# Zero columns beside a weight tile, so that every pass of p @ v loads 128 columns

## The chip, the core and the metric

The kernel runs on one core of a Trainium2 chip. The metric is the device time of one execution in microseconds (us); lower is better. TensorE multiplies matrices: it loads a tile of weights (LDWEIGHTS, shown in the profile as the engine PEld) and then streams a moving operand through it (MATMUL, shown as PE) into an accumulator in PSUM. VectorE (DVE), ScalarE (ACT) and GpSimd (POOL) work element by element, and SyncE (SP) issues the DMA transfers.

## The reference: windowed attention, then a softplus feed-forward

Inputs are q, k and v of shape (8, 8, 576, 64) and two weight matrices, all float32.

```python
scores = scale * np.matmul(q, k.transpose(0, 1, 3, 2))
mask = (rel >= 0) & (rel < 64)              # rel = query position - key position
attn = softmax(np.where(mask, scores, -1e9))
x = np.matmul(attn, v)                      # heads side by side: (4608, 512)
h = x @ w_in                                # 512 -> 2048
out = softplus(h) @ w_out                   # 2048 -> 512
```

A query sees its own key and the 63 before it, so a tile of 128 queries needs 192 keys.

## The kernel before

**Blocks and groups.** The 4608 tokens are cut into 12 blocks (*groups*) of 384 tokens (three tiles of 128). A sequence has 576 tokens, so some groups start a sequence and have no keys before them (`prev` is false). The attention of a group runs over four *head pairs* `hp`; each pair has two heads `hh` of 64 columns. The feed-forward of a group runs over 16 tiles `f` of the hidden width: `ffn_up` makes 12 products into `ps_h` (L403), softplus follows on ScalarE and VectorE (L407 to L414), and `ffn_down` makes 9 products into `ps_o` (L424). Both multiply float32 numbers that are split into two parts, three products of parts to each full one.

**Attention.** Groups 0 and 1 (in the kernel's own order) transpose the probabilities on TensorE and do everything in float32 (L255, L291, L349). The other ten groups, the ones that the change touches, go another way. Scores are products of split q and k (L259, four to a tile of queries). VectorE adds the mask and takes the minimum (L266), and ScalarE takes the exponential (L276). The probabilities p are divided by their sum (L284), then written as three bfloat16 parts p1 + p2 + p3 in the tile `nat` (L304 to L312), and two DMA transposes turn them into `tr` (L308, L313), which has keys on the partitions.

**p @ v in bfloat16 parts.** v is split in the same way, v1 + v2 + v3. Keys go through in chunks of 64, and 128 partitions hold a chunk twice. There are two sets of passes, `s = 0` and `s = 1`:

- `s = 0`: the moving operand has p1 in the upper 64 partitions and p2 in the lower ones. The weights `v12` have v1 in 64 columns and v2 in the 64 beside them, in both halves of the partitions. So the accumulator `av` gets (p1 + p2) v1 in its partitions 0 to 63, and (p1 + p2) v2 in partitions 64 to 127.
- `s = 1`: the moving operand has p3 above and p1 below. The weights `v13` have v1 above (L331) and v3 below (L330), in 64 columns. The result p3 v1 + p1 v3 belongs to partitions 0 to 63 alone, and before the change the product is written as a 64-column one.

A head has seven chunks (six where `prev` is false), so 14 (or 12) passes at L378, each with its own load of weights: over all, 80 heads, 1088 passes, half of them with `v13`. The inner chunks move 128 columns of `tr`, the first and the last chunk move 64. After the last pass, ScalarE and VectorE add the two halves of `av` (L383, L384), and the sum is split again into `x` (L386, L387), which `ffn_up` of the next group reads.

**What sets the order.** The stages of the attention are a generator; they and the steps of the feed-forward are put into one list of events with due times (`BASE`, `PACE`, `STG`, `DOWN`) and emitted in that order. Up to due time 100 a scheduler orders the instructions of every engine; from there on TensorE keeps the order in which the events were written, and the scheduler orders the other engines. In that part the 14 passes of a head stand together as a rule, and the four L259 products of a tile of the next head pair follow them.

Of the kernel before, what the change touches and what calls it, by code (L numbers as in the profile page):

```python
# [9 lines left out]
BF16 = mybir.dt.bfloat16  # L10
# [3 lines left out]
ALU = mybir.AluOpType  # L14

P = 128
# [5 lines left out]
NCH = TB // CH + 1  # L22
# [16 lines left out]
def window_attention_softplus_ffn(  # L39
# [24 lines left out]
    nc = tc.nc  # L64
# [11 lines left out]
    cpool = ctx.enter_context(tc.tile_pool(name="cpool", bufs=1))  # L76
    ld = ctx.enter_context(tc.tile_pool(name="ld", bufs=1))
    att = ctx.enter_context(tc.tile_pool(name="att", bufs=1))
# [35 lines left out]
    for t in kbd_s:  # L114
        nc.gpsimd.memset(t[D:P, 0, :], 0.0)
        nc.gpsimd.memset(t[0:D, 1, :], 0.0)
        nc.gpsimd.memset(t[0:D, 0, 0:CH], 0.0)
        nc.gpsimd.memset(t[D:P, 1, 0:CH], 0.0)
    v_pads = [att.tile([P, 2, NJ, 2, P], F32, name="v_pad", tag=n) for n in ("nat", "tr")]
    for t in v_pads:  # L120
        nc.vector.memset(t, 0.0)
# [59 lines left out]
    def attention(g, hp):  # L181
# [6 lines left out]
        def bank():  # L188
            if not odd0:
                return ps_a.tile([P, 512], F32, name="ps_a")  # L190

            taken_ps[0] += 1
            return ps_o.tile([P, 512], F32, name=f"ps_o{taken_ps[0] % NJ}")
# [40 lines left out]
        else:  # L234
            q_hl = att.tile([P, 2, TB], F32R, name="q_hl")
            low = heads[1]
# [48 lines left out]
        if by_pe:  # L285

            pt = att.tile([P, 2, TB], F32, name="pt", tag="q_hl")
            for hh in range(2):
                pp = bank()
                for j in range(NJ):  # L290
                    tp(pp[:, j * P : (j + 1) * P], sv[:, hh * NJ + j, 0:P], ident)  # L291
                (nc.vector.tensor_copy if hh else nc.scalar.copy)(pt[:, hh, :], pp[:, :TB])
        else:

            nat = att.tile([P, 2, 4 * NJ, 2, CH], BF16, name="nat")
            tr = att.tile([P, 8 * NJ, P], BF16, name="tr")
            pv = [pn.rearrange("p i (f c) -> p i f c", f=2), nat.rearrange("p s (i f) b c -> p s i f b c", f=2)]

            def part(s, b):
                return pv[1][:, s, :, :, b, :]  # L300

            n = 4 * NJ
            yield
            nc.scalar.copy(part(0, 0), pv[0])  # L304
            nc.vector.tensor_tensor(pv[0], pv[0], part(0, 0), ALU.subtract)  # L305
            yield
            nc.scalar.copy(part(0, 1), pv[0])  # L307
            nc.sync.dma_start(  # L308
                tr[:, 0:n, :], nat[:, 0, :, :, :].rearrange("p n b c -> p (n b c)"), transpose=True
            )  # L310
            nc.vector.tensor_tensor(part(1, 0), pv[0], part(0, 1), ALU.subtract)
            nc.vector.tensor_copy(nat[:, 1, :, 1, :], nat[:, 0, :, 0, :])  # L312
            nc.sync.dma_start(  # L313
                tr[:, n:, :], nat[:, 1, :, :, :].rearrange("p n b c -> p (n b c)"), transpose=True
            )
            yield
            v_in = att.tile([P, NCH, P], F32, name="v_in")
            for half in heads:
                nc.sync.dma_start(v_in[half, :, :], v[ks, c0 : c0 + P].rearrange("(c p) n -> p c n", p=CH))
            yield  # L320

            v12 = att.tile([P, NCH, 2, 2, D], BF16, name="v12")
            v13 = att.tile([P, NCH, 2, D], BF16, name="v13")
            vv = v_in.rearrange("p c (h d) -> p c h d", h=2)
            up, low = heads
            nc.scalar.copy(v12[:, :, :, 0, :], vv)  # L326
            nc.vector.tensor_tensor(vv, vv, v12[:, :, :, 0, :], ALU.subtract)  # L327
            yield
            nc.scalar.copy(v12[:, :, :, 1, :], vv)
            nc.vector.tensor_tensor(v13[low, :, :, :], vv[low, :, :, :], v12[low, :, :, 1, :], ALU.subtract)  # L330
            nc.vector.tensor_copy(v13[up, :, :, :], v12[up, :, :, 0, :])  # L331
        yield

        if hp == 0:
# [5 lines left out]
        if by_pe:  # L340
            av = bank()
# [3 lines left out]
        for hh in range(2):  # L345
            if by_pe:
                for a in range(2 * NJ):
                    cs = slice(a * CH, (a + 1) * CH)
                    mm(  # L349
                        av[:, cs], v_pad[:, a % 2, a // 2, hh, :], pt[:, hh, cs],  # L350
                        start=(hh == 0 and a == 0), stop=(hh == 1 and a == 2 * NJ - 1), skip_group_check=True,
                    )
                if hh == 1:
                    nc.scalar.copy(x_t[0], av[:, :TB])
                    nc.vector.tensor_tensor(x_t[1], av[:, :TB], x_t[0].bitcast(F32), ALU.subtract)
                yield
                continue
            av = bank()
            passes = []
            for s in range(2):  # L360
                for c in range(0 if prev else 1, NCH):


                    j = (c - 1) // 2
                    n = s * 4 * NJ + (hh * NJ + j) * 2
                    if c % 2:
                        src, o = trf[:, (n + 1) * P : (n + 2) * P], j * P
                    elif c == 0:
                        src, o = trf[:, (n + 2) * P : (n + 2) * P + CH], 0
                    elif c == NCH - 1:  # L370
                        src, o = trf[:, n * P + CH : (n + 1) * P], j * P + CH
                    else:
                        at = n * P + CH
                        src = trf[:, at : at + 2 * W].rearrange("p (a b) -> p a b", b=W)[:, :, 0:CH]
                        o = j * P + CH
                    passes.append((s, c, src, slice(o, o + (CH if c in (0, NCH - 1) else P))))
            for i, (s, c, src, osl) in enumerate(passes):
                mm(  # L378
                    av[: D if s else P, osl], v13[:, c, hh, :] if s else v12[:, c, hh, :, :], src,
                    start=(i == 0), stop=(i == len(passes) - 1), skip_group_check=True,  # L380
                )
            ds = heads[hh]
            nc.scalar.copy(xf[ds, :], av[D:P, :TB])  # L383
            nc.vector.tensor_tensor(xf[ds, :], av[0:D, :TB], xf[ds, :], ALU.add)  # L384
            if hh == 1:
                nc.scalar.copy(x_t[0], xf)  # L386
                nc.vector.tensor_tensor(x_t[1], xf, x_t[0].bitcast(F32), ALU.subtract)  # L387
            yield
# [68 lines left out]
    for g in range(NB):  # L457
        for hp in range(NP):
            if g < 3:
                base = BASE[g] + PACE[g] * hp  # L460
            else:
                base = 2 * NF * (g - 1) + SHP * hp + SH
            stages = attention(g, hp)
            for at in STG if g >= 2 else STG0:
                events.append((base + at, lambda stages=stages: next(stages, None)))
# [59 lines left out]
```

## Time and profile before

| What | Before |
|---|---|
| runs | 1057.53, 1059.34, 1063.11 us (median 1059.34) |
| the profiled execution | 1059.67 us, span 1057.9 us |
| TensorE busy with products | 1004.5 us (95%), 5888 of them |
| TensorE busy with loads | 883.0 us (83%) |
| VectorE busy | 813.9 us (77%) |
| ScalarE busy | 740.2 us (70%) |
| GpSimd busy | 54.4 us (5%) |
| L378, products / loads | 78.8 us / 60.3 us busy, 1088 each |

The span runs from the first to the last instruction of the program; 1.8 us of the execution's time lie outside it. A matmul's row reads `line PE MATMUL out<-in weights shape moving shape xcount`: `128*64 128x128` means weights on 128 partitions with 64 columns, and a moving operand with 128 columns. Products overlap in TensorE, so the length of one (about 0.2 us at L378) is not what a pass costs; that is the distance from the start of one to the start of the next. The chain of waits is the work that ended last, followed back from the end: each of its rows gives a start, the time by which that work moved the chain on, and how many instructions it merges. Rows in square brackets give idle time before an instruction and what ended it.

### The profile page before, as it was taken

What the parts mean: (1) busy time and instruction counts of PE and PEld (TensorE: products, weight loads), DVE (VectorE), ACT (ScalarE), POOL (GpSimd) and SP (SyncE); (2) the same over time, 40 slices, a digit from 0 to 9 for tenths busy, and PEclk for the clock granted to TensorE, in tenths of its full rate; (3) what the DMA queues carried; (4) which work ended last, traced back from release to release, by engine and by line L of the source; (5) the groups of instructions that cost most, each with busy time, mean ns of one, the idle gap of its engine ahead of it and who ended that gap; (6) DMA issues with size and microseconds to landing.
All of it is one profiled execution on the core that took longest, in us unless ns stands there. A gap on an engine that the chain in (4) does not pass through costs nothing.

```text
span 1057.9 us, 16725 instructions
## 1 busy us (share of the span) xinstructions
PE 1004.5 (95%) x5888; PEld 883.0 (83%) x5888; DVE 813.9 (77%) x1797; ACT 740.2 (70%) x1705; POOL 54.4 (5%) x53
## 2 busy tenths in 40 slices
PE   5768589999989999999999999999999999999998
PEld 3657488888778988888888888888888888888997
DVE  7889989667986778878877877877887887875322
ACT  4566479677776678778868877877877877865443
POOL 3233420000000000000000000000000000000000
PEclk8989769999999999999999999999999999999999
DMA  6576246344653436635534534534544554631000
GB/s 199 164 260 192 71 137 154 86 128 92 155 116 80 110 80 113 158 80 111 159 81 110 156 84 110 145 95 101 144 105 94 144 112 85 145 57 30 30 1 30
DMA packets 209748, 119.06 MB, mean 113 GB/s; under 512 B 143360, under 2 KB 201728, under 8 KB 208128
## 3 DMA queue, kind: packets, MB, share of 16 engines
q1 hardware_dynamic: 209664, 118.00, 45.0%
q8 instruction: 46, 0.75, 0.3%
q14 instruction: 38, 0.31, 0.1%
HBM read 76.28 MB, written 10.22 MB: 82 GB/s over the span
## 4 chain that ended last, share of the span: by engine, by line
PE 83%; DVE 10%; DMA 4%; ACT 1%; issue 1%; SPq 1%; ACTq 0%
PE ps_h L403 35%; PE ps_o L424 35%; PE ps_a L378 6%; PE ps_a L259 6%; DVE st L266 1%; DMA raws<-in_w_words_dram 1%; DVE ws L171 1%; DVE ws L170 1%; DVE st L284 1%; DMA v_in<-in_v_dram 1%; DVE ws L169 1%; DMA tr<-nat 1%; DMA kbd<-in_kT_dram 1%; DMA raw<-in_w_words_dram 1%; DVE ws L168 1%
## 5 line engine op out<-in xcount | busy, mean ns | idle before, releaser
L403 PE MATMUL ps_h<-x,w 128*128 128x384 f32 x2304 | 448.9, 342 | 9.4 <-DVE u L411 8.3
L424 PE MATMUL ps_o<-w,g 128*128 128x512 f32 x1728 | 436.4, 395 | 2.1 <-ACT g L413 2.1
L403 PEld LDWEIGHTS ps_h<-x,w 128*128 128x128 f32 x2304 | 406.8, 190 | 25.6 <-DVE u L411 11.0
L424 PEld LDWEIGHTS ps_o<-w,g 128*128 128x128 f32 x1728 | 319.2, 189 | 60.9 <-ACT g L413 2.7
L407 ACT ACTIVATE u<-ps_h 128x384 f32<-128x384 f32 x192 | 93.9, 489 | 135.3 <-PE ps_h L403 128.5
L411 DVE SCALAR_TENSOR_TENSOR u<-ps_h,u 128x384 f32<-128x384 f32 x192 | 106.2, 554 | 76.5 <-ACT u L409 75.3
L276 ACT ACTIVATE st<-st,mn 128x128 f32<-128x128 f32 x288 | 112.0, 390 | 17.7 <-DVE st L272 17.7
L414 DVE TENSOR_TENSOR g<-u,g 128x384 fp32r<-128x384 f32 x192 | 106.9, 558 | 12.0 <-ACT g L413 10.6
L266 DVE CUSTOM_DVE_ANT_0 st<-ps_a,mask 128x192 f32<-128x192 f32 x216 | 69.7, 352 | 58.5 <-PE ps_a L259 57.1
L408 ACT ACTIVATE u<-u 128x384 f32<-128x384 f32 x192 | 100.7, 526 | 3.3
L409 ACT ACTIVATE u<-u 128x384 f32<-128x384 f32 x192 | 100.3, 522 | 3.8
L378 PEld LDWEIGHTS <-v 128*128 128x128 bf16 (+1 forms) x1088 | 60.3, 104 | 30.8 <-issue 23.3
L378 PE MATMUL ps_a<-tr,v 128*64 128x128 bf16 (+3 forms) x1088 | 78.8, 215 | 3.3 <-DMA tr<-nat 3.3
L259 PE MATMUL ps_a<-k,q_hl 128*128 128x192 f32 x480 | 78.8, 288 | 0.0
L259 PEld LDWEIGHTS ps_a<-k,q_hl 128*128 128x128 f32 x480 | 67.2, 193 | 7.6
L413 ACT CAST g<-u 128x384 fp32r<-128x384 f32 x112 | 57.0, 509 | 21.6 <-DVE u L411 21.2
L307 ACT CAST nat<-st 128x768 bf16<-128x768 f32 x40 | 33.2, 831 | 38.3 <-DVE st L305 38.2
L383 ACT COPY xf<-ps_a 64x384 f32<-64x384 f32 x80 | 38.1, 476 | 25.6 <-PE ps_a L378 24.4
L276 ACT ACTIVATION_READ_ACCUMULATOR st<-st,mn 128x1 f32 x288 | 54.0, 188 | 0.0
L284 DVE TENSOR_TENSOR st<-st,sm 128x768 f32<-128x768 f32 x48 | 50.4, 1049 | 1.2
L384 DVE TENSOR_TENSOR xf<-ps_a,xf 64x384 f32<-64x384 f32 x80 | 43.8, 548 | 6.1 <-ACT xf L383 4.8
L327 DVE TENSOR_TENSOR v_in<-v_in,v 128x896 f32<-128x896 f32 x40 | 43.5, 1087 | 4.5 <-ACT v L326 4.5
(81 smaller groups left out, 885.7 us busy)
## 6 DMA issues: line engine op xcount, KB each, us to landing
k_in<-in_kT_dram SPq DMA_DIRECT2D x80, 224.0 KB, 3.8
v_in<-in_v_dram SPq DMA_DIRECT2D x80, 224.0 KB, 3.6
q_in<-in_qT_dram SPq DMA_DIRECT2D x84, 192.0 KB, 4.0
raws<-in_w_words_dram SPq DMA_DIRECT2D x12, 1024.0 KB, 5.7
out_dram<-raw SPq DMA_DIRECT2D x12, 512.0 KB, 2.8
raw<-in_w_words_dram SPq DMA_DIRECT2D x8, 512.0 KB, 5.3
out_dram<-raw SPq DMA_DIRECT2D x12, 256.0 KB, 2.6
v_pad<-in_v_dram SPq DMA_DIRECT2D x52, 32.0 KB, 2.7
```

The source lines that it names most:

```text
L259: mm(spv[:, hh, :], q_hl[:, hh, js], part[:, hh, kc], start=(hh == 0 and i == 0), stop=(hh == 1 and i == 1), skip_group_check=True,)
L266: nc.vector.tensor_tensor_reduce(st[:, hh, j, :], spv[:, hh, :], m, QSCALE, 3.0e38, ALU.add, ALU.min, mn[:, hh, j : j + 1])
L276: nc.scalar.activation(sv[:, i, 0:P], sv[:, i, 0:P], AF.Exp, bias=mn[:, hh, j : j + 1], scale=-1.0, accum_out=sm[:, i : i + 1])
L284: nc.vector.tensor_tensor(pn, pn, sm.unsqueeze(2).to_broadcast([P, 2 * NJ, P]), ALU.mult)
L378: mm(av[: D if s else P, osl], v13[:, c, hh, :] if s else v12[:, c, hh, :, :], src, start=(i == 0), stop=(i == len(passes) - 1), skip_grou ...
L403: mm(hv, weight(0, a, f)[:, c * P : (c + 1) * P], x[b][c], start=(i_mm == 0), stop=(i_mm == 3 * NC - 1))
L407: nc.scalar.activation(u, hv, AF.Abs)
L408: nc.scalar.activation(u, u, AF.Exp, scale=-1.0)
L409: nc.scalar.activation(u, u, AF.Ln, bias=1.0)
L411: nc.vector.scalar_tensor_tensor(gf, hv, 0.0, u, ALU.max, ALU.add)
L414: nc.vector.tensor_tensor(gt[1], gf, gt[0].bitcast(F32), ALU.subtract)
L424: mm(ops[g][j], gt[a][:, js], weight(1, b, f), start=(first and i == 0), stop=(last and i == 2),)
```

## The change

`v13` becomes one tile that lives as long as the kernel, with 128 columns for each chunk and head: 64 for v1 over v3, and 64 that are set to zero once, by GpSimd, at the start of the program. VectorE writes the first 64 columns for every head pair, as before. The passes of `s = 1` take all 128 columns and write all 128 partitions of `av`; the zero columns add nothing to partitions 64 to 127.

```diff
+    v13 = cpool.tile([P, NCH, 2, 2, D], BF16, name="v13")
+    nc.gpsimd.memset(v13, 0.0)
...
             v12 = att.tile([P, NCH, 2, 2, D], BF16, name="v12")
-            v13 = att.tile([P, NCH, 2, D], BF16, name="v13")
...
-            nc.vector.tensor_tensor(v13[low, :, :, :], vv[low, :, :, :], v12[low, :, :, 1, :], ALU.subtract)
-            nc.vector.tensor_copy(v13[up, :, :, :], v12[up, :, :, 0, :])
+            nc.vector.tensor_tensor(v13[low, :, :, 0, :], vv[low, :, :, :], v12[low, :, :, 1, :], ALU.subtract)
+            nc.vector.tensor_copy(v13[up, :, :, 0, :], v12[up, :, :, 0, :])
...
                 mm(
-                    av[: D if s else P, osl], v13[:, c, hh, :] if s else v12[:, c, hh, :, :], src,
+                    av[:, osl], (v13 if s else v12)[:, c, hh, :, :], src,
                     start=(i == 0), stop=(i == len(passes) - 1), skip_group_check=True,
                 )
```

In the changed kernel, lines up to 118 keep their numbers, lines 119 to 323 move by 3, and lines from 325 on by 2 (L378 becomes L380).

The order on TensorE, ScalarE and SyncE is the same in both programs, instruction for instruction, and what VectorE's instructions at L330 and L331 wait for is the same too. Three places matter. The first is TensorE in the middle of a head, where the last pass with `v12` meets the first passes with `v13`. Before (the numbers in the names tell buffers apart; a product's size is weights' columns by moving columns):

```order
L378 LDWEIGHTS v_7037
L378 MATMUL ps_a<-tr,v_7037 128x64
L378 LDWEIGHTS v_7038
L378 MATMUL ps_a<-tr,v_7038 64x64
L378 LDWEIGHTS v_7038
L378 MATMUL ps_a<-tr,v_7038 64x128
```

and with the change:

```order
L380 LDWEIGHTS v_7015
L380 MATMUL ps_a<-tr,v_7015 128x64
L380 LDWEIGHTS v_99
L380 MATMUL ps_a<-tr,v_99 128x64
L380 LDWEIGHTS v_99
L380 MATMUL ps_a<-tr,v_99 128x128
```

Nothing has moved here; the width of the second set is 128 in place of 64, and its tile is the one kept buffer. The second place is GpSimd at the start of the program. Before:

```order
L118 MEMSET kbd 64x64
L127 MEMSET mask 128x192
masks.py:197 MEMSET ident 128x128
L128 ISA
L128 AFFINE_SELECT mask<-mask 128x192
```

and with the change:

```order
L118 MEMSET kbd 64x64
L121 MEMSET v_99 128x1792
L130 MEMSET mask 128x192
masks.py:197 MEMSET ident 128x128
L131 ISA
L131 AFFINE_SELECT mask<-mask 128x192
```

The new memset stands behind the memsets of `kbd` and ahead of everything that makes the masks (`mask`, `mask_c`, `mask_b`) and the identity. The third place is VectorE's first work on scores (L266, now L269; each is followed by a read of its minimum). Before:

```order
L121 MEMSET v_pad 128x1536 x2
L266 ISA st,mn<-ps_a,mask_c 128x192
L266 ISA mn 128x1
L266 ISA st,mn<-ps_a,mask_c 128x192
L266 ISA mn 128x1
L266 ISA st,mn<-ps_a,mask 128x192
```

and with the change:

```order
L124 MEMSET v_pad 128x1536 x2
L269 ISA st,mn<-ps_a,mask 128x192
L269 ISA mn 128x1
L269 ISA st,mn<-ps_a,mask 128x192
L269 ISA mn 128x1
L269 ISA st,mn<-ps_a,mask_c 128x192
```

The two instructions with `mask`, for the second tile of queries, now come ahead of the two with `mask_c`, for the first tile. VectorE has one more difference: the first L284 of the program, which stood between two L266 of the next head pair, now stands behind both.

## The prediction

> **What bounds the kernel now.** I read busy time by stage first, then the chain of waits in each stage, then the passes of L378 in that chain. Busy time in two stretches (us; then the granted clock of TensorE, the share of the DMA engines, GB/s):
>
> ```profile
> core 0: us, PE busy (x) PEld busy (x) DVE busy (x) ACT busy (x) POOL busy (x), PEclk, DMA share, GB/s
> ...
> 305.00:980.00 675.00, 675.00 (x4111) 599.66 (x4110) 535.65 (x1211) 503.35 (x1150) 0.00 (x0) 1.00 0.47 108
> 980.00:1058.00 78.00, 73.66 (x366) 65.93 (x365) 24.53 (x46) 31.91 (x62) 0.00 (x0) 0.99 0.06 21
> ```
>
> From 305 to 980 us TensorE's products cover all of the 675 us, at a granted clock of 1.00, while VectorE has work for 79% and ScalarE for 75%. The last stage, with the feed-forward alone, has the same clock (0.99). The chain of waits says the same. Its shares by line, for 142 to 249.5, for 249.5 to 305 and for 305 us to the end:
>
> ```profile
> by line: PE ps_h L403 43.9%; PE ps_o L424 41.5%; PE ps_a L259 6.6%; PE ps_a L378 6.4%; ACT wh L167 0.6%; DVE st L266 0.5%; DVE u L411 0.4%; DVE wh L168 0.4%; issue 0.1%; DVE mn L266 0.0%
> by line: DMA v_in<-in_v_dram 14.1%; DMA tr<-nat 11.1%; DVE v L330 5.7%; issue 5.2%; PE ps_h L403 4.8%; DVE k L244 4.7%; DVE st L266 4.6%; DVE v_in L327 3.6%; DVE q_hl L238 3.5%; DVE u L411 3.4%; DVE nat L311 3.3%; PE ps_o L424 3.0%; DVE x L
> by line: PE ps_o L424 42.8%; PE ps_h L403 42.8%; PE ps_a L378 7.0%; PE ps_a L259 6.9%; DVE raw L443 0.1%; issue 0.0%
> ```
>
> So TensorE's own pace sets the time from 142 to 249.5 and from 305 us on. In between, DMAs and VectorE do; time that TensorE saves there is waited away. How many of the 544 passes with 64 columns lie in each stretch (142 to 249.5, 249.5 to 305, 305 to 980):
>
> ```profile
> L378 PEld LDWEIGHTS <-v 128*64 128x64 bf16 x56 | 3.2, 109 | 2.6 <-issue 1.9 <-DVE sm L281 0.4
> L378 PEld LDWEIGHTS <-v 128*64 128x64 bf16 x42 | 2.5, 109 | 4.5 <-issue 4.3
> L378 PEld LDWEIGHTS <-v 128*64 128x64 bf16 x446 | 25.5, 110 | 6.1 <-issue 1.1
> L378 PEld LDWEIGHTS <-v 128*128 128x128 bf16 x446 | 23.8, 98 | 14.1 <-issue 13.9 <-DMA tr<-nat 0.2
> L378 PE MATMUL ps_a<-tr,v 128*64 128x128 bf16 x330 | 30.0, 221 | 0.0
> L378 PE MATMUL ps_a<-tr,v 128*128 128x128 bf16 x330 | 29.4, 220 | 0.0
> ```
>
> The first stretch has 8 heads and the second 6, seven passes each. The third has 66: a head has five inner chunks, and 330 / 5 = 66.
>
> **The change on TensorE.** Sixty-four columns more do not make a pass longer: a 128-column load takes 98 ns against 110, and a product 220 ns against 221. What differs is what happens where the width changes. Pieces of the chain (start, time on the chain), first a head with both widths, then seven passes with 128 columns alone, then seven with 64 columns alone; behind them TensorE's loads at a head of each kind:
>
> ```profile
> 411.52 0.81 PE ps_a L378 x14
> 412.33 0.62 PE ps_a L259 x4
> ...
> 181.15 0.35 PE ps_a L378 x7
> 181.50 0.51 PE ps_a L259 x4
> ...
> 191.06 0.46 PE ps_a L378 x7
> ```
> ```profile
> 712.48 0.37 PEld L378 LDWEIGHTS <-v 128*128 128x128 bf16 x7 [0.28 <-issue]
> 712.92 0.39 PEld L378 LDWEIGHTS <-v 128*64 128x64 bf16 x7
> 713.38 0.52 PEld L259 LDWEIGHTS ps_a<-k,q_hl 128*128 128x128 f32 x4
> ...
> 180.99 0.37 PEld L378 LDWEIGHTS <-v 128*128 128x128 bf16 x7 [0.26 <-ACT u L409]
> 181.31 0.53 PEld L259 LDWEIGHTS ps_a<-k,q_hl 128*128 128x128 f32 x4
> ```
>
> At 180.99 the seven loads with 128 columns are followed by L259's first load after 0.32 us. At 712.48 the same seven are followed by the first 64-column load only after 0.44 us, and the seven 64-column ones by L259's after 0.46 us. On the chain, seven 128-column passes take 0.35 us and the four L259 behind them 0.51. Seven 64-column passes take 0.46, and the L259 behind a full head 0.62. So each change of width, into 64 or out of it, costs about 0.11 us, whether the neighbour is bfloat16 or float32; from 128-column bfloat16 to 128-column float32 (181.5) there is no such pause. A head with its four L259 now takes 0.81 + 0.62 = 1.43 us; with one width it is 0.35 + 0.35 + 0.51 = 1.21 us. **Gain: 0.22 us a head.**
>
> - 305 us on: 66 x 0.22 = 14.5 us, all on the chain.
> - 142 to 249.5: 8 x 0.22 = 1.8 us, on the chain, which leaves TensorE at 249.5 for VectorE.
> - 249.5 to 305: 6 x 0.22 = 1.3 us, waited away. Taken as 0; bounds 0 and 1.3.
>
> A rule of the Trainium skill speaks against this change: its page "TensorE: Matmul & The Clock Gate", section LDWEIGHTS, has the time of a load grow with its columns (columns / 1.2 in ns), so 53 ns for 64 and 107 ns for 128, and an estimate by that figure is 544 x 53 ns = 29 us more of loads. The rows above disagree (110 against 98 ns). The same page's section on weight-path modes exempts it: loads of 128 columns that are not float32 get a fast mode. By that one the sum stands; by the first, see the slower rival.
>
> **The change elsewhere.** VectorE writes the same elements, now 64 in every 128. The nearest rows write bfloat16 in just that stride (L312, L311):
>
> ```profile
> L331 DVE COPY v<-v 64x896 bf16<-64x896 bf16 x40 | 15.2, 380 | 0.5 <-PE ps_a L378 0.4
> L312 DVE COPY nat<-nat 128x768 bf16<-128x768 bf16 x40 | 14.1, 353 | 0.0
> L330 DVE TENSOR_TENSOR v<-v_in,v 64x896 bf16<-64x896 f32 x40 | 43.6, 1089 | 1.2
> L311 DVE TENSOR_TENSOR nat<-st,nat 128x768 bf16<-128x768 f32 x40 | 38.2, 956 | 5.7 <-ACT nat L307 5.5
> ```
>
> Per element that is 0.42 against 0.46 ns for the copies and 1.22 against 1.24 ns for the subtractions, so the stride costs nothing I can see; the bound is 10% of 380 ns, 40 times, on an engine with 20% to spare. The kept tile adds no wait: `v13` had one buffer before as well.
>
> The memset of 1792 columns is priced from two others, and its cover from the first uses of the masks and, later, of L284:
>
> ```profile
> 3.24 0.27 POOL L127 MEMSET mask<- 128x192 bf16 x1
> 5.22 0.15 POOL L137 MEMSET mask_c<- 128x64 bf16 x1
> 6.14 0.36 DVE L266 CUSTOM_DVE_ANT_0 st<-ps_a,mask_c 128x192 f32<-128x192 f32 x1 [2.07 <-PE ps_a L255]
> 7.30 0.36 DVE L266 CUSTOM_DVE_ANT_0 st<-ps_a,mask 128x192 f32<-128x192 f32 x1 [0.52 <-PE ps_a L255]
> 8.57 0.36 DVE L266 CUSTOM_DVE_ANT_0 st<-ps_a,mask 128x192 f32<-128x192 f32 x1 [0.63 <-PE ps_a L255]
> 17.09 1.81 DVE L284 TENSOR_TENSOR st<-st,sm 128x768 f32<-128x768 f32 x1
> 19.05 0.85 PE L291 MATMUL ps_a<-ident,st 128*128 128x128 f32 x6
> ```
>
> From 0.15 us for 64 columns and 0.27 for 192, a column costs 0.94 ns, and 1792 columns 0.27 + 1600 x 0.94 ns = 1.8 us. `mask_c`, finished at 5.37, comes at 7.2. The new order uses `mask` first, when its product is there (7.30), then `mask_c` from 7.86 to about 8.5, and the third tile at 8.57 as before. So the 1.8 us are hidden by TensorE's slow first products; without that cover they cost 1.8 us. Behind the masks GpSimd has nothing until 15 us. L284 now stands behind one more L266 (0.36 us), and six transposes (19.05) wait for it: 0 to 0.4 us later, I take 0.2.
>
> **Sum.** 14.5 + 1.8 - 0.2 = 16.1 us off the profiled execution's 1059.67 gives 1043.6 us. That execution lay 0.3 us above the median of the runs shown, which makes 1043.3; I say **1043.5 us**. Its own range is 1040 (all 80 heads, and the heads cut in two by other work, which change width more often) to 1047.
>
> **The rivals.**
>
> A. *Slower: the zero-padded tile loads as slowly as float32 weights do.* Four L259 passes, 128 columns each, take 0.51 us, 0.128 a pass; seven `v13` passes would take 0.90, and a head with its L259 0.35 + 0.90 + 0.51 = 1.76 in place of 1.43. On 74 heads that is 24 us: 1084 us. It decides once a `v13` pass costs more than (0.46 + 0.11) / 7 = 0.081 us. Against it: `v12`, with the same type and the same 128 columns side by side, loads in 98 ns and passes in 0.05 us. The rule on LDWEIGHTS of the Trainium skill's page "TensorE: Matmul & The Clock Gate" would lead here; by the loads of `v12` the trace does not follow it.
>
> B. *Half: the pause at a head's end comes from going from bfloat16 to float32, not from the width.* Then only the one inside the head goes: 74 x 0.11 = 8.1 us, 1051.5 us. For it: every head's end has both changes at once. Against it: the passage at 181.5, without a pause.
>
> C. *Other waits take the place.* The nearest one in 305 to 980 us:
>
> ```profile
> PEld ps_h L403 <- DVE x L387: 1.1, 7, 0.2
> ACT u L407 <- PE ps_h L403: 86.4, 72, 2.6
> DVE st L266 <- PE ps_a L259: 79.4, 58, 2.3
> ```
>
> Loads of L403 already wait for `x` at seven places; each would grow by up to the 0.11 us that TensorE comes earlier, 0.8 us. With the 1.8 us of the early heads lost to the VectorE stretch at 250 as well, 1046.2 us. Much more I doubt, since ScalarE and VectorE wait for TensorE 86 and 79 us in that stage.
>
> D. *Nothing*: TensorE's time comes back as a longer stretch from 250 to 305 and later starts: 1055 us or more. Nothing in the rows speaks for it.
>
> **Chances.** Forecast 0.70, C 0.15, B 0.07, D 0.04, A 0.04. The range 1039.5 to 1050 holds the forecast and C, about 0.85. Faster by over 0.5% (under 1054; 0.5% is about what a measurement can tell from no change) is 0.70 + 0.15 + 0.07 = 0.92, the same 0.04, slower 0.04.
>
> **What would show it.** The page shows 1088 products at L380 all with 128 columns, loads near 98 ns. On the chain a head of 14 passes takes 0.70 us, the four L259 behind it 0.51, and the stretch from 305 us to the end is 14.5 us shorter. B shows as L259 still at 0.62, A as 1.25 us a head. C shows as idle TensorE ahead of L403. The memset shows as 1.8 us on GpSimd with VectorE's third tile still at about 8.6 us. I am wrong if the pauses stay though the widths are equal.

## The result: 1042.3 us, 1.6% faster, as forecast

| | Before | Changed |
|---|---|---|
| median | 1059.82 us (4 runs, 1057.53 to 1063.11) | 1042.34 us (4 runs, 1041.65 to 1044.23) |
| ratio, with its 95% interval | | 0.9836 [0.9806, 0.9865] |
| the profiled execution | 1059.67 us, span 1057.9 | 1044.23 us, span 1042.4 |

The forecast was 1043.5 us, in a range of 1039.5 to 1050. Busy time of the changed kernel, by the same stages (columns as before: us, granted clock, share of the DMA engines, GB/s):

```profile
250.00:305.00 55.00, 48.59 (x302) 41.73 (x301) 48.22 (x108) 41.63 (x98) 0.00 (x0) 0.97 0.57 135
305.00:980.00 675.00, 675.00 (x4191) 607.74 (x4190) 541.53 (x1222) 511.88 (x1168) 0.00 (x0) 1.00 0.47 109
```

The first of these stretches in the kernel before:

```profile
250.00:305.00 55.00, 49.42 (x310) 42.09 (x310) 49.40 (x112) 42.94 (x104) 0.00 (x0) 1.00 0.57 137
```

The shares by line of the changed kernel's chain of waits, from 305 us to the end:

```profile
by line: PE ps_o L426 42.8%; PE ps_h L405 42.7%; PE ps_a L380 5.9%; PE ps_a L262 5.9%; DVE raw L445 0.1%; issue 0.0%
```

TensorE still covers all of the long stage, at the same clock, and does 4191 products in its 675 us where it did 4111. The passes of p @ v have gone from 7.0% of the chain to 5.9%, and the L259 (now L262) products behind them from 6.9% to 5.9%. Pieces of that chain at the two heads of one head pair, and TensorE's loads at the first of them:

```profile
449.06 0.69 PE ps_a L380 x14
449.75 0.51 PE ps_a L262 x4
450.26 2.11 PE ps_h L405 x12
452.37 0.69 PE ps_a L380 x14
453.06 0.51 PE ps_a L262 x4
```
```profile
448.90 0.70 PEld L380 LDWEIGHTS <-v 128*128 128x128 bf16 x14 [0.28 <-issue]
449.56 0.53 PEld L262 LDWEIGHTS ps_a<-k,q_hl 128*128 128x128 f32 x4
```

A head takes 0.69 us in place of 0.81, its four L262 0.51 in place of 0.62: 1.20 us in place of 1.43. These pieces are typical: from start to start, all 43 whole heads from 305 us on that have four L262 right behind them take 1.19 us, and took 1.43. The fourteen loads run through in one piece, and L262's first load starts 0.66 us after the head's first, where the kernel before had 0.90 (712.48 to 713.38). The loads of the whole line, before and after, with shortest, median and longest in ns, and the first and the last start (the counts by width at the end of a row are those of every sixth load):

```profile
L378 PEld LDWEIGHTS <-v x1088: 95/104/113, 164.3 to 975.9; 128*128 128x128 bf16 x100, 128*64 128x64 bf16 x82
```
```profile
L380 PEld LDWEIGHTS <-v x1088: 95/98/102, 166.0 to 960.5; 128*128 128x128 bf16 x182
```

Between the first pass of p @ v and the last lie 811.6 us before and 794.5 us now, 17.1 us less. Ahead of the first the profiled execution lost 1.7 us, and behind the last nothing changed (82.0 and 81.9 us to the end of the span).

To see where the time went I followed single products of TensorE, since their order is the same in both programs. The last column is a second profile of the changed kernel, that of the run r6_after_again below.

| Stretch, from the start of one product to the start of another | Forecast | Before | Changed | Changed, again |
|---|---|---|---|---|
| span's start to the 541st | +0.2 | 155.04 us | 156.74 | 156.30 |
| 541st to 1141st (at 257 us) | -1.8 | 101.84 | 99.25 | 99.22 |
| 1141st to 1441st (at 308 us) | 0 | 50.95 | 52.40 | 50.95 |
| 1441st to the last | -14.5 | 745.44 | 729.41 | 729.33 |

### The profile page after: what moved, and what is told of

Its sections match the earlier page's. It is cut to its first block, busy times and chain, and to the rows that moved or that the text cites. A ratio compares the mean times of both kernels' runs of the same rounds, so it can differ in the third digit from the quotient of the medians.

```text
span 1042.4 us, 16725 instructions
## 1 busy us (share of the span) xinstructions
PE 990.4 (95%) x5888; PEld 879.7 (84%) x5888; DVE 812.8 (78%) x1797; ACT 740.3 (71%) x1705; POOL 56.0 (5%) x54
## 4 chain that ended last, share of the span: by engine, by line
PE 71%; DVE 2%; DMA 1%; ACT 1%; issue 0%; SPq 0%; ACTq 0%; DVEq 0%
PE ps_h L405 31%; PE ps_o L426 31%; PE ps_a L380 4%; PE ps_a L262 4%; DMA tr<-nat 1%; DMA v_in<-in_v_dram 0%; DVE st L269 0%; DVE v L332 0%; DVE raw L443 0%; DVE u L413 0%; DVE nat L314 0%; DVE k L247 0%; ACT nat L310 0%; DVE g L416 0%; DVE xf L386 0%
## 5 line engine op out<-in xcount | busy, mean ns | idle before, releaser
L269 DVE CUSTOM_DVE_ANT_0 st<-ps_a,mask 128x192 f32<-128x192 f32 x216 | 69.7, 352 | 49.4 <-PE ps_a L262 45.8
L262 PE MATMUL ps_a<-k,q_hl 128*128 128x192 f32 x480 | 77.3, 285 | 0.0
L380 PEld LDWEIGHTS <-v 128*128 128x128 bf16 x1088 | 56.1, 98 | 23.9 <-issue 22.1
L380 PE MATMUL ps_a<-tr,v 128*128 128x128 bf16 (+1 forms) x1088 | 70.1, 213 | 3.4 <-DMA tr<-nat 3.4
L262 PEld LDWEIGHTS ps_a<-k,q_hl 128*128 128x128 f32 x480 | 67.6, 195 | 3.4
```

The source lines that it names most:

```text
L262: mm(spv[:, hh, :], q_hl[:, hh, js], part[:, hh, kc], start=(hh == 0 and i == 0), stop=(hh == 1 and i == 1), skip_group_check=True,)
L269: nc.vector.tensor_tensor_reduce(st[:, hh, j, :], spv[:, hh, :], m, QSCALE, 3.0e38, ALU.add, ALU.min, mn[:, hh, j : j + 1])
L380: mm(av[:, osl], (v13 if s else v12)[:, c, hh, :, :], src, start=(i == 0), stop=(i == len(passes) - 1), skip_group_check=True,)
```

## The experiments

Theory: TensorE pauses for about 0.11 us whenever the number of weight columns goes from 128 to 64 or back, and the change takes those pauses away; nothing else in it matters. Rivals: that the shorter loads of full-width weights (98 against 110 ns) are what gains; that going between types (bfloat16, float32) or between the two sets of passes is what pauses; that the kept tile does it.

**Everything but the width.** The changed kernel, with the passes of `s = 1` back at 64 columns.

```diff
-                    av[:, osl], (v13 if s else v12)[:, c, hh, :, :], src,
+                    av[: D if s else P, osl], v13[:, c, hh, 0, :] if s else v12[:, c, hh, :, :], src,
```

> The kept, padded and zeroed tile as in the change, but the v13 passes read its first 64 columns only and write 64 partitions as before the change. Width theory (each change between 64 and 128 weight columns pauses TensorE by 0.11 us, all else in the change is free): no gain, 1058 to 1062 us; a head of 14 passes stays at 0.81 us on the chain and the four L259 behind it at 0.62. Rival (the gain comes from the kept tile, the stride of its writes or the later masks): 1042 to 1050 us.

Measured: 1059.88 us, ratio to the kernel before 1.0009 [0.9994, 1.0025]. Its chain at a head:

```profile
450.56 0.81 PE ps_a L380 x14
451.37 0.62 PE ps_a L262 x4
```

The pauses are all there, and so is the time. The kept tile, its zeros, the later masks and the strided writes give nothing; what they cost together is at most the upper end of the interval, 0.25% or 2.6 us.

**The dose: the passes of a head alternate between the two tiles.** Once in the kernel before (64 and 128 columns in turn), once in the changed kernel (128 throughout). Both have the same edit:

```diff
+            passes.sort(key=lambda e: e[1])
             for i, (s, c, src, osl) in enumerate(passes):
```

> The kernel before, with the passes of a head sorted by chunk: v12 and v13 passes alternate, widths 128 and 64 in turn. A head then has 14 changes of width in place of 2 (12 in place of 2 where it has no keys before it). Width theory: 12 more pauses of 0.08 to 0.11 us for each of about 74 heads on the chain, 71 to 98 us more: 1130 to 1158 us. Rival (the pause belongs to the end of a set of passes, not to the width): 1059 to 1065 us.

> The changed kernel with the passes of a head sorted by chunk: v12 and v13 alternate, all with 128 columns. Width theory: the order costs nothing, 1041 to 1045 us. Rival (changing the weight tile itself costs something): up to the 71 to 98 us of the other alternating kernel.

Measured: 1157.98 us, ratio 1.0929 [1.0896, 1.0962], with alternating widths, at the upper end of what was expected; 1043.53 us, ratio 0.9848 [0.9819, 0.9877], with one width. The chain at a head, first with alternating widths (L378 is L379 there), then with one (L381):

```profile
457.04 2.15 PE ps_a L379 x14
459.19 0.62 PE ps_a L259 x4
```
```profile
447.49 0.69 PE ps_a L381 x14
448.18 0.51 PE ps_a L262 x4
```

With no change of width a head and its L259 take 1.20 us, with two 1.43 us, with fourteen 2.77 us. That is 0.115 us a change from the first step and (2.77 - 1.20) / 14 = 0.112 us from the whole: each change costs the same, however often it comes. Over the whole kernel, 1080 changes in place of 174 make 1157.98 us out of 1058.72, 0.11 us each. Alternating between two weight tiles costs nothing as long as the widths are equal, so it is not the tile and not the end of a set of passes.

**How wide is wide enough.** 96 and 72 of the 128 columns used, that is 32 and 8 zero columns (the edit for 72 has 72 in both places).

```diff
-                    av[:, osl], (v13 if s else v12)[:, c, hh, :, :], src,
+                    av[: 96 if s else P, osl],
+                    v13.rearrange("p c h i d -> p c h (i d)")[:, c, hh, 0:96] if s else v12[:, c, hh, :, :], src,
```

> The padded tile, with 96 of its 128 columns used: 32 zero columns beside the 64. Theory M (the pause belongs to a switch between a 64-column setting of the array and the full one; 96 columns need the full one): no pauses; a pass costs between 0.056 us (its load hidden as now) and 0.08, so 1043 us, up to 1043 + 74 heads x 7 x 0.025 us = 1056 us. Theory W (any change in the number of columns pauses): the pauses stay, a head at 0.81 us, 1058 us or more. Theory F (loads without the fast form pause against bfloat16 loads that have it): the pause inside a head stays, the one at its end goes, 1051 us.

> As the kernel with 96 columns, with 72: only 8 zero columns beside the 64. If the array has a 64-column setting and a full one, and every width above 64 takes the full one: no pauses, a head of 14 passes at 0.69 to 0.72 us and L259 at 0.51, 1042 to 1045 us. If the settings are finer (the pause comes back below some width between 64 and 96): a head at 0.81 and L259 at 0.62, 1058 to 1061 us.

Measured: 1043.26 us, ratio 0.9852 [0.982, 0.9884], with 96 columns; 1041.82 us, ratio 0.9842 [0.9807, 0.9877], with 72. For 96 columns the chain at a head, and the loads as groups (mean length behind the busy time, in ns); then the same for 72:

```profile
451.23 0.72 PE ps_a L380 x14
451.95 0.51 PE ps_a L262 x4
```
```profile
L380 PEld LDWEIGHTS <-v 128*96 128x96 bf16 x544 | 36.0, 125 | 5.5 <-issue 4.2
L380 PEld LDWEIGHTS <-v 128*128 128x128 bf16 x544 | 29.0, 98 | 17.9 <-issue 15.9 <-DMA tr<-nat 1.4 <-ACT v L331 0.5
```
```profile
446.28 0.70 PE ps_a L380 x14
446.98 0.51 PE ps_a L262 x4
```
```profile
L380 PEld LDWEIGHTS <-v 128*72 128x72 bf16 x544 | 33.1, 114 | 4.2 <-issue 2.8
```

Neither has a pause, inside a head or at its end, although its loads are longer than the ones with 64 columns (125 and 114 against 110 ns). So the theory needs narrowing: it is not any change in the number of columns, since 128 to 96 and 128 to 72 are free. What pauses is the step between 64 columns and a width from 72 up. The shorter load of the full width is not the gain either: against 96 columns it is worth 0.03 us a head, an estimated 2 us over the 66 heads from 305 us on, and against 72 columns 0.01 us. From the 1441st product to the last, 72 columns take 729.7 us and 128 columns 729.4, against 745.4 before. The kernel with 96 columns has some 115 of its products in other places in the order, so its 732.3 us can't be laid beside these, and its verdict rests on the heads.

That fits a rule of the Trainium skill, on its page "TensorEngine Tiling (Array Packing)", section Key Properties: changing the tiling mode drains TensorE. The modes that the page lists under Available Configurations have 128, 64 or 32 columns. The traces are in keeping with it: 0.11 us for a step between 128 and 64 columns in either direction, and 72 and 96 columns on the side of 128. No run here shows that the pause is such a drain, or what 32 columns do.

**The zeros written later.** GpSimd writes only the 64 zero columns, behind the masks, and VectorE's first work is in its old order.

```diff
-    nc.gpsimd.memset(v13, 0.0)
...
+    for i in range(2):
+        nc.gpsimd.tensor_scalar(
+            v13[:, :, i, 1, :], mask_b[:, 0:D].unsqueeze(1).to_broadcast([P, NCH, D]), 0.0, None, ALU.mult
+        )
```

> The changed kernel with the zero columns written later: no memset ahead of the masks; GpSimd writes only the 64 zero columns, as mask_b times 0, behind mask_b. VectorE's first work has the order of the kernel before again. If the memset is hidden, as the prediction has it: same time as the changed kernel run beside it, within 1 us. Rival (the memset costs its 1.6 us, or the opening's 1.7 us that the changed kernel's profile lost by 155 us): 1.5 to 2 us less than the changed kernel.

> The changed kernel unaltered, for a comparison on one chip with the version that writes the zeros later: 1041 to 1045 us, ratio to the kernel before 0.982 to 0.986.

Measured: 1042.4 us, ratio 0.9829 [0.9807, 0.9852], with late zeros; 1042.22 us, ratio 0.9833 [0.9816, 0.9851], with the memset ahead of the masks. They can't be told apart, as the prediction had it. The intervals leave room for 2 us either way, though, and the start of the 541st product doesn't settle it: it lies between 154.2 and 156.7 us in the six profiles of kernels with the early memset, and is at 152.0, 152.7 and 155.0 us in the three without it. Earlier places in the traces narrow this down. TensorE's seventh product, which ends 6.4 to 6.6 us of waiting for a DMA, starts at 15.05 and 14.96 us in the two profiles of the changed kernel and at 15.15 before, and the 221st at 65.24 and 65.66 against 65.46. So by 65 us nothing is left of what the memset may have held up. What makes the opening differ behind that stays open.

No version beat the changed kernel by more than the runs can tell.

## Why the prediction was right, step by step

**The bound.** Right. TensorE's pace sets the time from 142 to 249.5 and from 305 us on, and saved time came out whole there. From 257 to 308 us, where the forecast had the gain waited away, the second profile has 50.95 us as before, and the first 1.45 us more. All of this lies between the 1361st and the 1381st product (293.0 to 297.5 us): there the first profile has a granted clock of 0.84 (290 to 295 us) and 0.82 (295 to 300), and the other two have 1.00. Up to the 1361st product the three are level, at 37.0 to 37.1 us from the 1141st. Such a dip (0.78 from 290 to 295 us) stands in the kernel with alternating widths too, so it is not tied to equal widths.

**The price of a change of width.** Right in kind, and 0.22 us a head was 0.23. It rested on three passages of the trace before: seven 128-column passes ahead of float32 products (0.35 us, no pause), and the two pauses of a full head. The alternating kernel confirms it with seven times as many changes to a head.

**The sum.** The last stage gave 16.0 us and not 14.5, the stage from 155 to 257 us 2.6 and not 1.8. Both the price of a change and the number of changes were too small. I counted heads, two changes to each: 66 and 8. A head that other work cuts inside its 64-column passes has four, which I had only in the lower end of the range. Counted one by one in the trace before, the width changes 136 times from 305 us on, not 132, and 22 times from 142 to 249.5, not 16. At 0.115 us each that is 15.6 and 2.5 us. In the last stage the price explains 0.7 us of the difference and the number 0.5, which leaves 0.4 us unexplained; in the earlier stretch nearly all of it is the number.

That the total came within 1.2 us of the forecast is in part luck. The two stages gave 2.3 us more than forecast, and the opening took back 1.7 us in the first profile and 1.3 in the second, where 0.2 were forecast.

**Costs at nothing.** The memset took 1.60 us (1.8 forecast), and VectorE's third tile of queries came at 8.64 (8.57 before), as the forecast worked out. L284 cost nothing that lasted. The six transposes behind it start at 19.02 us (19.05 before), since L284 itself took 1.30 us in place of 1.81. TensorE's next product then starts at 20.44 in place of 20.14, but at 23.83 it is level again (23.80 before).

```profile
3.24 1.60 POOL L121 MEMSET v<- 128x1792 bf16 x1
7.48 0.36 DVE L269 CUSTOM_DVE_ANT_0 st<-ps_a,mask 128x192 f32<-128x192 f32 x1 [3.41 <-PE ps_a L258]
8.64 0.36 DVE L269 CUSTOM_DVE_ANT_0 st<-ps_a,mask 128x192 f32<-128x192 f32 x1
17.26 1.30 DVE L287 TENSOR_TENSOR st<-st,sm 128x768 f32<-128x768 f32 x1
19.02 1.46 PE L294 MATMUL ps_a<-ident,st 128*128 128x128 f32 x6
```

The strided writes cost nothing, as the nearest rows said (380 and 1089 ns before):

```profile
L332 DVE TENSOR_TENSOR v<-v_in,v 64x896 bf16<-64x896 f32 x40 | 43.6, 1090 | 1.2
L333 DVE COPY v<-v 64x896 bf16<-64x896 bf16 x40 | 15.2, 379 | 0.0
```

**The rivals.** A fell: `v13` loads in the same 98 ns as `v12`. B fell: L262 stands at 0.51 us wherever the passes take 72 columns or more, and the pause at a head's end went with the width. C did not come about. The loads that wait for `x` in 305 to 980 us did not grow, and ScalarE still waits for TensorE most of all:

```profile
ACT u L409 <- PE ps_h L405: 88.9, 76, 2.6
PEld ps_h L405 <- DVE x L389: 1.1, 7, 0.2
```

D has in its favour the 1.7 us of the opening and the 1.45 us at the lower clock, in an execution that was the slowest of its four and still 15.4 us faster than the profiled one before.

## What to carry to other kernels

Where one engine sets the time, look for passages of the same work with and without the suspected cost in the trace that you have: seven passes of 0.35 us beside seven of 0.46 told this result before it was run. On TensorE, products with 64 columns of weights between products with 128 cost a pause at both ends; a few zero columns, eight here, buy it off if PSUM has the partitions to spare. Count the places where the price is paid, rather than the units of the program that usually hold two of them.

## What the runs showed of the hardware that I had not expected

- The pause depends on which side of a step between 64 and 72 columns the weights lie, not on their number: 128 to 96 and 128 to 72 columns go on without a gap.
- Loads of 64, 72 and 96 bfloat16 columns last 110, 114 and 125 ns in the profile, and those of 128 columns 98 ns: the widest is the shortest. From 64 to 96 columns that is 0.47 ns a column, less than the 0.83 (1 / 1.2) of the Trainium skill's page "TensorE: Matmul & The Clock Gate", section LDWEIGHTS; the measurement decides here.
- These differences hardly reach the end: a head takes 0.69, 0.70 or 0.72 us with 128, 72 or 96 columns.
